# A written-out order of 1,052 steps changed in many small places, one unit's transposes moved to the DMA crossbar, and 18 idle memsets on GpSimd

## The chip, the cores and the metric

One Trainium2 chip, one core of it. The metric is the device time of the program in microseconds, as the median of several runs. One profiled execution of the kernel before is at hand, with a record of every instruction and DMA.

## The reference

Four sequences of 768 positions, 8 heads of 64. First attention in a window of 128 positions, with the first 4 positions ("sinks") always seen; then a channel mix (an FFN with a gate) on the heads laid side by side (512 wide).

```python
scores = scale * np.matmul(q, k.transpose(0, 1, 3, 2))
keep = is_sink | in_window          # rel in [0, 128), or position < 4
a = softmax(np.where(keep, scores, -1e9))
x = np.matmul(a, v)                 # then heads side by side: [4, 768, 512]

x_prev = x shifted by one position
xk = mu_k * x + (1.0 - mu_k) * x_prev
xr = mu_r * x + (1.0 - mu_r) * x_prev
k = np.maximum(xk @ w_k, 0.0)       # 512 -> 1024
v = k * k @ w_v                     # 1024 -> 512
r = 1.0 / (1.0 + np.exp(-(xr @ w_r)))
out = r * v
```

## The kernel before

**Units.** The work is cut into 12 units of 256 positions, three to a sequence (`u = 3 * b + T`). Each unit goes through the same steps. `load` brings k, q and v from HBM (two DMAs of 256 KB each) on the queue of SP. `prepare` casts k, q and v to bf16 and transposes k and q: with PE (`transpose`, then an `evacuate` copy out of PSUM by ACT or DVE) in the first units, with a DMA transpose on SP's queue (`turn`) where `KD` and `QD` say so, k from unit 4 and q from unit 8. `attend` makes the scores on PE in two pairs of head pairs, takes their exp on ACT (`expo`), multiplies by the window mask on DVE (`masked`; units 0 and 1 add a bias on PE instead), and multiplies by v on PE (`values`, 16 matmuls of 65 columns with two head pairs); DVE divides (`rec`, a reciprocal, and `x`). `sink_scores`, `es` and `sink_values` are the same for the four sink positions, whose keys GpSimd copies out of kt with `sink_keys` once a sequence. `mix` transposes x (`xtp` on PE and a copy, or two DMA transposes for the units in `XD`), forms the shifted difference `td` and from it `xk` and `xr` (four `stt` of 256 columns each). `ffn` of a unit makes `keys` (8 halves of 4 matmuls), `relu`, `square`, `gate` (2 of 4 matmuls, and a tanh), `product` (4 of 4 matmuls) and the output, which SP stores.

**What sets the order.** Nothing is scheduled at run time. Every step is put down with `P.op` under a running number. `ORDER` lists these numbers in the order in which the steps are issued; an engine runs its own steps in this order and waits for each. Numbers below zero are fillers: a matmul of 512 zero columns into a bank (`warm`, L1018), which nobody reads. `CHOICE` gives, by number, the engine for the steps that ACT, DVE or GpSimd can do. `SLOTS` gives, for each buffer taken, which of a pool's buffers it is. Weights are loaded whole (`load_weight`), and cast to bf16 by ACT or DVE (the `emit` steps for `wk`, `wr`, `wv`).

**Lines used below.** L337, L317, L307: loads of q and k (by 8 rows of descriptors or plain) and v; L354: weights; L536, L543: casts of k and q; L646: cast of v; L576: PE transposes of k and q; L589: their copies to kt and qt; L562: the DMA transposes `turn`; L670: `sink_keys`; L680: sink values; L703, L775: the two exps; L721, L728: scores and bias; L808: `values`; L849, L858, L869: x by PE, its copy, x by DMA; L877, L888: difference and mixes; L939, L979, L997, L909: `keys`, `gate`, `product`, the last product; L1006, L919: outputs; L1013: stores; L501: weight casts.

Of the kernel before, what the change touches and what calls it, by code (L numbers as in the profile page):

```python
# [8 lines left out]
FP32 = mybir.dt.float32  # L9
# [9 lines left out]
    92: "ACT", 93: "ACT", 94: "ACT", 95: "ACT", 97: "ACT", 100: "ACT", 102: "DVE", 105: "DVE",  # L19
    110: "DVE", 111: "DVE", 114: "ACT", 115: "DVE", 139: "POOL", 142: "POOL", 145: "POOL", 148:  # L20
    "DVE", 150: "DVE", 151: "ACT", 152: "ACT", 154: "DVE", 161: "DVE", 191: "DVE", 193: "DVE",
    194: "DVE", 197: "DVE", 199: "DVE", 200: "DVE", 203: "DVE", 204: "DVE", 213: "DVE", 230:
    "ACT", 234: "ACT", 273: "DVE", 276: "DVE", 279: "DVE", 282: "DVE", 285: "ACT", 286: "ACT",
    298: "DVE", 306: "DVE", 315: "ACT", 354: "DVE", 364: "ACT", 365: "DVE", 367: "DVE", 383:
    "ACT", 387: "ACT", 436: "DVE", 439: "DVE", 444: "DVE", 445: "DVE", 467: "ACT", 475: "ACT",
    514: "DVE", 516: "DVE", 521: "DVE", 524: "ACT", 525: "ACT", 546: "ACT", 550: "ACT", 554:
    "ACT", 558: "ACT", 595: "DVE", 598: "DVE", 603: "ACT", 604: "ACT", 606: "DVE", 634: "ACT",
    681: "DVE", 682: "DVE", 691: "DVE", 700: "ACT", 704: "ACT", 708: "ACT", 755: "DVE", 759:
    "DVE", 760: "ACT", 772: "DVE", 781: "ACT", 785: "ACT", 789: "ACT", 834: "DVE", 836: "DVE",
    837: "DVE", 853: "ACT", 856: "DVE", 857: "ACT", 860: "DVE", 861: "ACT", 904: "DVE", 906:  # L30
    "DVE", 910: "DVE", 912: "DVE", 913: "DVE", 929: "ACT", 933: "ACT", 940: "DVE", 941: "ACT",
    994: "DVE", 995: "ACT", 999: "ACT", 1003: "ACT", 1007: "ACT", 1022: "DVE", 1026: "DVE",
    1034: "DVE", 1035: "ACT",
# [5 lines left out]
XD = (9,10,11)  # L39
# [146 lines left out]
def kernel(  # L186
# [14 lines left out]
    nc = tc.nc  # L201
# [326 lines left out]
    def prepare(u, rank):  # L528
        b, T = divmod(u, NT)
# [545 lines left out]
```

## Time and profile before

| what | value |
|---|---|
| median of 3 runs | 166.04 us (165.84 to 166.12) |
| profiled execution, first to last instruction (span) | 164.3 us |
| own time of that execution, with what lies around the span | not given by itself; the median is 1.74 us above the span |
| PE busy (matmuls) | 158.4 us, 96% |
| DVE busy | 145.4 us, 89% |
| ACT busy | 131.2 us, 80% |
| GpSimd (POOL) busy | 13.5 us, 8% |
| mean granted TensorE clock | 0.999 |
| moved by DMA | 34.60 MB, mean 211 GB/s |

A busy share says how much of the span an engine worked, not whether anyone waited for it. A matmul's busy time holds the way through the array, so that matmuls close behind each other overlap and a busy PE can still have waits in it; the chain that ended last shows start to start instead. SPq stands for the queue of DMAs that SP issues, in order; such an instruction's length is the time of issue, and the landing comes later.

### The profile page before, as it was taken

To read this page: it belongs to the slowest core of one execution; us is meant where nothing else is said; L and a number is where in the kernel's file an instruction comes from. 1 tells how busy PE (TensorE), PEld (TensorE's weight loads), DVE (VectorE), ACT (ScalarE), POOL (GpSimd) and SP (SyncE) were. 2 spreads that over 40 slices of the span, in tenths; PEclk is the share of its full clock that TensorE was granted. 3 is DMA by queue.
4 is the path that set the end of the run, shared out by engine and by line. 5 is a ranking of instruction groups with operands and counts; after the bars stand their busy time and mean duration, and the time that the engine had idled before them with its cause. 6 is when DMAs were issued, how large, how long until landed. Compare 5 with 4: busy or idle time off the path is not lost.

```text
span 164.3 us, 4195 instructions
## 1 busy us (share of the span) xinstructions
PE 158.4 (96%) x1603; PEld 102.6 (62%) x1603; DVE 145.4 (89%) x381; ACT 131.2 (80%) x218; POOL 13.5 (8%) x38
## 2 busy tenths in 40 slices
PE   6999889999999999999999999999999999999992
PEld 2455568866467587577566775856575765664851
DVE  5259999999999999989999999999999999789752
ACT  3277999999999999999999999997668759163240
POOL 6409300010000000060000000000000000000000
PEclk9999999999999999999999999999999999999999
DMA  4999999999969896999999887986996955077743
GB/s 120 247 305 311 348 335 355 301 354 210 228 154 270 135 240 148 234 198 167 224 216 157 188 156 163 235 146 150 199 123 136 362 149 200 0 90 297 262 185 128
DMA packets 79042, 34.60 MB, mean 211 GB/s; under 512 B 67112, under 2 KB 73520, under 8 KB 79024
## 3 DMA queue, kind: packets, MB, share of 16 engines
q1 hardware_dynamic: 79008, 34.35, 86.3%
q8 instruction: 12, 0.20, 0.6%
q14 instruction: 6, 0.05, 0.1%
q10 hardware_dynamic: 16, 0.00, 0.0%
HBM read 24.12 MB, written 6.29 MB: 185 GB/s over the span
## 4 chain that ended last, share of the span: by engine, by line
PE 79%; ACT 8%; SPq 4%; DMA 3%; issue 2%; DVE 1%; POOL 1%; DVEq 0%; ACTq 0%; POOLq 0%
PE bank L997 23%; PE bank L939 23%; PE bank L979 12%; PE bank L808 6%; PE sc L721 6%; SPq L337 3%; DMA qs<-in_q_dram 3%; PE bank L576 2%; ACT e L775 2%; PE bank L849 2%; ACT rl L949 1%; PE bank L763 1%; ACT qt L589 1%; PE bank L909 1%; PE bank L1018 1%
## 5 line engine op out<-in xcount | busy, mean ns | idle before, releaser
L775 ACT ACTIVATE e<-sc 128x1024 bf16<-128x1024 f32 (+1 forms) x48 | 46.1, 994 | 1.8 <-PE sc L721 1.7
L939 PE MATMUL bank<-xk,wk_sb 128*128 128x256 bf16 x384 | 47.1, 273 | 0.0
L997 PE MATMUL bank<-wv_h,kk 128*128 128x512 bf16 x184 | 43.1, 379 | 0.1
L939 PEld LDWEIGHTS <-wk_sb 128*128 128x128 bf16 x384 | 36.4, 98 | 7.4 <-issue 0.4
L949 ACT ACTIVATE rl<-bank 128x512 bf16<-128x512 f32 x40 | 24.2, 625 | 8.6 <-PE bank L939 7.1
L997 PEld LDWEIGHTS <-kk 128*128 128x128 bf16 x184 | 17.1, 98 | 17.8 <-issue 0.4
L789 DVE TENSOR_TENSOR e<-e,mask 128x1024 bf16<-128x1024 bf16 (+1 forms) x40 | 25.4, 642 | 0.7 <-ACT e L775 0.5
L979 PE MATMUL bank<-wr_sb,xr 128*128 128x512 bf16 x96 | 23.7, 379 | 0.0
L888 DVE SCALAR_TENSOR_TENSOR xk<-td,mu_all,xt 128x256 bf16<-128x256 bf16 x48 | 22.4, 483 | 0.3
L888 DVE SCALAR_TENSOR_TENSOR xr<-td,mu_all,xt 128x256 bf16<-128x256 bf16 x48 | 22.1, 475 | 0.2
L967 ACT ACTIVATE kk<-rl 128x512 bf16<-128x512 bf16 x29 | 18.3, 664 | 4.2 <-DVE rl L953 4.0
L985 ACT ACTIVATE th<-bank 128x512 f32<-128x512 f32 x24 | 15.1, 646 | 5.7 <-PE bank L979 5.7
L825 DVE TENSOR_TENSOR x<-bank,rec 128x256 bf16<-128x256 f32 x48 | 19.2, 416 | 0.4
L808 PE MATMUL bank<-vb,e 128*128 128x65 bf16 x352 | 16.6, 194 | 0.0
L1006 DVE SCALAR_TENSOR_TENSOR w<-th,bank 128x512 f32<-128x512 f32 x19 | 13.0, 682 | 3.6 <-issue 1.8
L808 PEld LDWEIGHTS <-e 128*128 128x128 bf16 x352 | 13.6, 97 | 3.5
L979 PEld LDWEIGHTS <-xr 128*128 128x128 bf16 x96 | 8.8, 98 | 8.6 <-issue 0.2
L721 PE MATMUL sc<-qt,kt 64*128 64x128 bf16 (+1 forms) x256 | 13.9, 238 | 0.0
L721 PEld LDWEIGHTS <-kt 64*128 64x128 bf16 x256 | 8.9, 94 | 5.7 <-issue 3.1
L1018 PE MATMUL bank<-warm 128*128 128x512 bf16 x30 | 10.6, 484 | 1.1 <-DVE warm L1038 1.1
L877 DVE TENSOR_TENSOR td<-xt 128x512 bf16<-128x512 bf16 x24 | 10.3, 428 | 0.7 <-ACT xt L858 0.5
L589 ACT COPY qt<-bank 128x512 bf16<-128x512 bf16 x15 | 9.4, 643 | 1.0 <-PE bank L576 1.0
(74 smaller groups left out, 161.7 us busy)
## 6 DMA issues: line engine op xcount, KB each, us to landing
ks<-in_k_dram SPq DMA_DIRECT2D x24, 256.0 KB, 4.7
qs<-in_q_dram SPq DMA_DIRECT2D x24, 256.0 KB, 4.4
vs<-in_v_dram SPq DMA_DIRECT2D x24, 256.0 KB, 4.4
out_dram<-w SPq DMA_DIRECT2D x19, 256.0 KB, 2.7
w<-in_moe_w_k_dram SPq DMA_DIRECT2D x2, 1024.0 KB, 10.4
w<-in_moe_w_v_dram SPq DMA_DIRECT2D x2, 1024.0 KB, 9.3
w<-in_moe_w_r_dram SPq DMA_DIRECT2D x1, 1024.0 KB, 9.7
out_dram<-ob SPq DMA_DIRECT2D x4, 256.0 KB, 2.6
```

What stands on the lines that cost most here:

```text
L721: nc.tensor.matmul(out=sc[:, a, o0:o1], lhsT=lhs[rows], rhs=rhs[rows], start=u not in BIAS, stop=True, skip_group_check=u in BIAS)
L775: nc.scalar.activation(out=buf[ek][:, :, lo:], in_=buf[sck][:, :, lo:], func=AF.Exp, scale=scale)
L789: nc.vector.tensor_tensor(out=at, in0=at, in1=m, op=ALU.mult)
L808: nc.tensor.matmul(out=o[:, g, a, :], lhsT=e[:, a, e0:e0 + 128], rhs=rhs, start=(T == 0 and i == 0), stop=(i == len(blocks) - 1), skip_gro ...
L825: P.op("DVE", dve(256), lambda ok=ok, rk=rk, c=c: nc.vector.tensor_tensor(out=buf["x", u][:, :, 128 * c:128 * c + 128].rearrange("p g (a d ...
L888: nc.vector.scalar_tensor_tensor(out=buf[key][:, c, :], in0=buf[tk][:, i, :], scalar=mu[w][:, c:c + 1], in1=xt[:, c, t0 - 1:t0 + 255], op0 ...
L939: nc.tensor.matmul(out=ps[:, i, :], lhsT=wk_sb[:, c, 128 * f:128 * f + 128], rhs=xk[:, c, :], start=(c == 0), stop=(c == NC - 1), skip_gro ...
L949: nc.scalar.activation(out=buf[rk], in_=buf[psk].rearrange("p (i t) -> p i t", i=2), func=AF.Relu)
L967: nc.scalar.activation(out=buf["kk", u][:, 2 * f2:2 * f2 + 2, :], in_=buf[rk], func=AF.Square)
L979: nc.tensor.matmul(out=buf[psk], lhsT=buf["xr", u][:, c, 128 * g:128 * g + 128], rhs=wr_sb[:, c, :], start=(c == 0), stop=(c == NC - 1))
L985: P.op("ACT", act(512), lambda psk=psk, tk=tk: nc.scalar.activation(out=buf[tk], in_=buf[psk], func=AF.Tanh, scale=0.5), rank + 4 + g, tak ...
L997: nc.tensor.matmul(out=buf[psk], rhs=wv_h[:, f, :], lhsT=buf["kk", u][:, f, 128 * g:128 * g + 128], start=(f == 0), stop=(f == NF - 1))
```

## The change

Three things are changed.

1. `XD` goes from units 9, 10, 11 to units 8 to 11: x of unit 8 is transposed by two DMA transposes in place of two packs of four PE transposes with a copy each. That makes 1,050 steps of 1,052.
2. `ORDER`, `CHOICE` and `SLOTS` are replaced. Decoded to step names: 19 fillers in place of 30. In units 0 and 1, q is loaded ahead of k, and the steps of q stand ahead of those of k. Before unit 0's first `keys`, the new order has the first score pair of unit 2, the second half of unit 1's x transposes and the second half of unit 2's k transposes, which came after it; unit 2's sink scores came before and come after. Engines change for 60 steps: v of units 0 and 1 and a part of q of unit 1 go to GpSimd (5 casts); counted over all, ACT has 225 steps in place of 219, DVE 356 in place of 369. Loads move by a few places on SP's queue; v of unit 11's first half is loaded much earlier. Near the end, the last `values` (unit 11) stand ahead of both gates and all products of unit 9; both gates of unit 11 stand ahead of its keys, and the four products of unit 10 behind them.
3. `sink_keys` of the second sequence (unit 3) is followed by 18 memsets of one column each into a tile that nothing reads.

```diff
 CHOICE = {
-    92: "ACT", 93: "ACT", 94: "ACT", 95: "ACT", 97: "ACT", 100: "ACT", 102: "DVE", 105: "DVE",
...
+    92: "DVE", 93: "ACT", 94: "ACT", 95: "ACT", 96: "DVE", 97: "ACT", 98: "DVE", 99: "DVE", 100:
+    "ACT", 101: "DVE", 102: "DVE", 104: "ACT", 105: "DVE", 107: "ACT", 108: "ACT", 110: "DVE",
+    111: "ACT", 113: "ACT", 114: "POOL", 115: "POOL", 139: "POOL", 141: "ACT", 142: "POOL", 144:
+    "ACT", 145: "POOL", 147: "ACT", 148: "POOL", 150: "ACT", 151: "POOL", 152: "POOL", 154: "DVE",
...
-XD = (9,10,11)
+XD = (8, 9, 10, 11)
...
 ORDER = (
-    80, 81, 78, 82, 87, 83, 84, 77, -1, -2, -3, -4, -1, -2, 90, 0, 1, 79, 102, 108, -2, -3, -4,
-    -2, -3, -4, -2, 103, 104, 2, 3, 119, 105, -3, -4, 106, 107, 109, 110, 4, 5, 114, -2, -2, -2,
-    120, 121, 115, -2, -3, -4, -2, -3, 122, 111, 112, 123, 124, 125, 126, 127, 129, 113, 130,
...
+    80, 82, 83, 87, 86, 77, 2, 85, 3, 0, 1, 4, 5, 81, 88, 114, 78, -1, -2, -3, -4, -1, 119, 8, 79,
+    105, -2, -3, -4, 106, 102, 107, 111, 89, 115, -4, -2, -3, -4, -1, 112, 108, -3, -4, 103, 104,
+    -4, -1, 120, 109, 121, -3, 90, 91, 117, 118, 125, 113, 122, 123, 110, 9, 129, 84, 126, 130,
...
+    spare = tile1([128, 18], FP32, "spare")
...
             for a in range(2):
                 rows = slice(64 * a, 64 * a + 64)
                 nc.gpsimd.tensor_copy(out=kz[rows, :, 4 * a:4 * a + NS],
                                       in_=first(rows))
+            if b == 1:
+                for i in range(18):
+                    nc.gpsimd.memset(spare[:, i:i + 1], 0.0)
```

More of the change, by code (lines that the diff above doesn't have):

```diff
@@ L18 @@
 CHOICE = {
-    92: "ACT", 93: "ACT", 94: "ACT", 95: "ACT", 97: "ACT", 100: "ACT", 102: "DVE", 105: "DVE",
[L20 to L30, printed above, removed]
@@ L31 @@
-    "DVE", 910: "DVE", 912: "DVE", 913: "DVE", 929: "ACT", 933: "ACT", 940: "DVE", 941: "ACT",
-    994: "DVE", 995: "ACT", 999: "ACT", 1003: "ACT", 1007: "ACT", 1022: "DVE", 1026: "DVE",
-    1034: "DVE", 1035: "ACT",
+    92: "DVE", 93: "ACT", 94: "ACT", 95: "ACT", 96: "DVE", 97: "ACT", 98: "DVE", 99: "DVE", 100:
+    "ACT", 101: "DVE", 102: "DVE", 104: "ACT", 105: "DVE", 107: "ACT", 108: "ACT", 110: "DVE",
+    111: "ACT", 113: "ACT", 114: "POOL", 115: "POOL", 139: "POOL", 141: "ACT", 142: "POOL", 144:
@@ new lines @@
+    "ACT", 145: "POOL", 147: "ACT", 148: "POOL", 150: "ACT", 151: "POOL", 152: "POOL", 154: "DVE",
+    161: "DVE", 191: "DVE", 193: "ACT", 194: "DVE", 196: "ACT", 197: "DVE", 199: "ACT", 200:
+    "ACT", 202: "ACT", 203: "DVE", 204: "DVE", 206: "DVE", 213: "DVE", 221: "ACT", 222: "ACT",
+    225: "DVE", 226: "DVE", 229: "ACT", 230: "ACT", 233: "DVE", 234: "DVE", 273: "DVE", 275:
+    "ACT", 276: "DVE", 278: "ACT", 279: "DVE", 281: "ACT", 282: "DVE", 284: "ACT", 285: "ACT",
+    286: "ACT", 291: "ACT", 298: "ACT", 306: "ACT", 307: "DVE", 310: "ACT", 311: "DVE", 314:
@@ new lines @@
+    "ACT", 315: "ACT", 318: "ACT", 319: "DVE", 354: "DVE", 356: "ACT", 358: "ACT", 359: "ACT",
+    361: "ACT", 363: "ACT", 364: "ACT", 365: "ACT", 367: "DVE", 374: "ACT", 382: "ACT", 383:
+    "ACT", 386: "ACT", 387: "DVE", 390: "ACT", 391: "DVE", 394: "ACT", 395: "DVE", 434: "ACT",
+    436: "DVE", 438: "ACT", 439: "DVE", 441: "ACT", 443: "ACT", 444: "DVE", 445: "DVE", 447:
+    "ACT", 454: "DVE", 462: "ACT", 463: "ACT", 466: "ACT", 467: "ACT", 470: "ACT", 471: "DVE",
+    474: "ACT", 475: "ACT", 514: "DVE", 516: "DVE", 518: "ACT", 519: "ACT", 521: "ACT", 523:
@@ new lines @@
+    "ACT", 524: "DVE", 525: "DVE", 530: "DVE", 537: "ACT", 545: "ACT", 546: "ACT", 549: "ACT",
+    550: "ACT", 553: "ACT", 554: "ACT", 557: "ACT", 558: "ACT", 593: "DVE", 595: "DVE", 597:
+    "ACT", 598: "DVE", 600: "ACT", 602: "ACT", 603: "ACT", 604: "ACT", 606: "ACT", 613: "ACT",
+    621: "ACT", 622: "ACT", 625: "ACT", 626: "DVE", 629: "ACT", 630: "DVE", 633: "ACT", 634:
+    "DVE", 673: "ACT", 675: "ACT", 677: "DVE", 679: "ACT", 681: "DVE", 682: "ACT", 684: "ACT",
+    691: "DVE", 699: "ACT", 700: "DVE", 703: "ACT", 704: "ACT", 707: "DVE", 708: "DVE", 711:
@@ new lines @@
+    "ACT", 712: "DVE", 751: "ACT", 753: "ACT", 755: "ACT", 757: "ACT", 759: "ACT", 760: "ACT",
+    778: "ACT", 779: "DVE", 782: "ACT", 783: "ACT", 786: "ACT", 787: "ACT", 790: "ACT", 791:
+    "ACT", 826: "DVE", 828: "ACT", 830: "DVE", 832: "ACT", 834: "ACT", 835: "ACT", 850: "ACT",
+    851: "ACT", 854: "ACT", 855: "DVE", 858: "ACT", 859: "ACT", 862: "ACT", 863: "ACT", 902:
+    "ACT", 904: "ACT", 906: "ACT", 908: "DVE", 910: "DVE", 911: "ACT", 926: "ACT", 927: "ACT",
+    930: "ACT", 931: "ACT", 934: "ACT", 935: "ACT", 938: "ACT", 939: "ACT", 992: "ACT", 993:
@@ L34 @@
+    "ACT", 996: "ACT", 997: "ACT", 1000: "DVE", 1001: "DVE", 1004: "ACT", 1005: "ACT", 1020:
+    "ACT", 1021: "ACT", 1024: "DVE", 1025: "DVE", 1028: "ACT", 1029: "ACT", 1032: "ACT", 1033:
+    "DVE",
 }
```

151 rows, old and new, of tables (ORDER, SLOTS) are left out of this document.

## The prediction

> **What bounds the kernel now.** I read the page's busy shares first, then busy time by stretch, then the chain that ended last, then instructions in order of time at both ends.
>
> ```profile
> span 164.3 us, 4195 instructions
> PE 158.4 (96%) x1603; PEld 102.6 (62%) x1603; DVE 145.4 (89%) x381; ACT 131.2 (80%) x218; POOL 13.5 (8%) x38
> ```
>
> ```profile
> 8.00:16.00 8.00, 7.70 (x84) 4.36 (x82) 5.65 (x17) 5.98 (x11) 3.36 (x6) 1.00 1.06 305
> 16.00:24.00 8.00, 7.04 (x113) 4.67 (x113) 7.93 (x24) 7.69 (x13) 1.87 (x8) 1.00 1.10 343
> 24.00:32.00 8.00, 8.00 (x88) 6.92 (x88) 7.79 (x21) 8.00 (x13) 0.00 (x0) 1.00 1.07 319
> 60.00:73.00 13.00, 12.94 (x153) 9.48 (x150) 12.25 (x31) 12.94 (x24) 2.50 (x2) 1.00 0.89 192
> 120.00:130.00 10.00, 10.00 (x96) 6.50 (x95) 9.76 (x23) 6.78 (x12) 0.00 (x0) 1.00 0.76 195
> 150.00:161.00 11.00, 11.00 (x76) 7.14 (x73) 7.38 (x15) 2.91 (x5) 0.00 (x0) 1.00 0.54 202
> ```
>
> The stretch table's columns are the stretch, its length, busy time of PE, PEld, DVE, ACT and POOL, the granted clock, the DMA share, GB/s. From 24 us to the end PE is busy 8.00 of 8.00, 10.00 of 10.00, 11.00 of 11.00; the weakest stretch, 60 to 73, still has 12.94 of 13.00. There is nothing to win there except less PE work. ACT is just as full up to 73 and then empties (6.78 of 10, 2.91 of 11). Only the first 24 us have room on PE.
>
> ```profile
> 7.97 4.54 DMA qs<-in_q_dram
> 12.64 0.88 POOL qb L543
> ...
> 18.51 0.59 ACT kt L589
> 19.10 0.29 ACT es L703
> 19.39 0.48 ACT qt L589
> ...
> 20.33 0.88 issue
> ...
> 24.13 0.90 PE bank L939 x8
> 25.03 0.22 PE bank L849 x4
> 25.25 0.22 PE bank L576 x4
> ...
> 26.47 0.55 PE sc L721 x12
> ...
> 157.63 1.73 PE bank L997 x8
> 159.36 1.76 PE bank L909 x16
> 161.15 0.42 DVE w L919
> ```
>
> This is the chain that ended last (start, length, what). Up to 24.13 it walks through the DMA of unit 1's q, a GpSimd cast and ACT copies, so the opening is bound by arrivals and by the in-order queues of ACT, DVE and GpSimd. From 24.13 (first FFN product, `keys`) PE carries nearly all of it, to 161.15. The rest, 3.1 us, is the last DVE operation and the store. The span is 164.3 and the median of the runs 166.04; I take the 1.74 between them as fixed. So the time moves with two things: when PE starts its FFN work, and how much PE work and PE waiting lie behind that.
>
> **The change part by part.**
>
> *Fillers.* The new order has 19 filler matmuls instead of 30.
>
> ```profile
> 1.13 2.74 PE L1018 MATMUL bank<-warm 128*128 128x512 bf16 x6 [1.13 <-DVE warm L1038]
> 4.17 3.03 PE L1018 MATMUL bank<-warm 128*128 128x512 bf16 x7
> 9.97 1.25 PE L1018 MATMUL bank<-warm 128*128 128x512 bf16 x5
> 16.68 1.94 ACT L775 ACTIVATE e<-sc 128x1024 bf16<-128x1024 f32 x2 [0.31 <-PE sc L721]
> 21.84 0.29 PE L696 MATMUL bank<-qt,ksink 128*32 128x256 bf16 x4 [0.50 <-ACT qt L589]
> 22.85 1.08 ACT L501 ACTIVATE wk_sb<-w 128x1024 bf16<-128x1024 f32 x1
> ```
>
> One filler takes 0.22 us late (5 in 1.25, with the pipeline's tail) and 0.43 early (7 in 3.03): the array starts at half rate and is at full rate by about 7 us, though the granted-clock column says 1.00 throughout. The new order keeps 18 ahead of unit 0's `values`, so the warm-up stays; those left out stood after it, in time when PE waits anyway: 0 us for the work itself. The cover that is lost is activity: gaps like the 0.50 in the row above will be longer, up to about 1 us, the length of one exp (1.94 for two). The upper end is a slow-clock rival below; I take 0. [...]
>
> *Work moved ahead of the first FFN product.* Before, the transposes of x of unit 1's second half (0.22, at 25.03), of k of unit 2's second half (0.22) and the first score pair of unit 2 (0.55) come behind the first `keys`. In the new order all three come ahead, and unit 2's sink scores (four matmuls; its packs of four cost PE the 0.22 of the other packs of four) go behind. PE work behind the first FFN product: -0.22 - 0.22 - 0.55 + 0.22 = **-0.77 us**.
>
> *x of unit 8 by the crossbar.* Two packs of four PE transposes go: **-0.44 us** of PE, and two ACT copies with them. SP gets two DMA transposes. Their price on SP and their delay are those of units 9 to 11:
>
> ```profile
> L869 SPq DMA_TRANSPOSE xt<-x x6: 1189/1230/2405, 117.3 to 144.0; - x6
> DMA to landing us min/median/max: 2.5/3.5/4.2
> ```
>
> 1.23 us of issue each. Between unit 8's last `values` and its first `keys` the new order lays 13 us of PE work (11.2 before); the way now needed is about 2.5 (reciprocals and x) + 5.1 (both transposes, from the tail below) + 2.3 for the first operations on DVE: it fits. Queued behind these transposes on SP are the loads of q and k of unit 11 and of v of unit 10; unit 11's k transposes follow behind unit 9's x transposes as well, and by the median landing they are down about 1.3 us before unit 11's scores are due (2.7 before). I take 0, with a rival.
>
> *The first units, q ahead of k.* The whole opening is changed: q0, k0, v0, q1, k1 are loaded in this order (before k0, q0, v0, half of k1, q1, rest of k1), v0 and v1 and all four casts of unit 1 go to GpSimd, and DVE and ACT get other pieces. Unit 1's q has one 256 KB load less ahead of it: at the 305 GB/s of the stretch 8 to 16 that is 0.9 us on its landing at 12.5 (an estimate). Its transposes feed the first exp of unit 1, at 16.68; I take 0.5 us earlier. From that exp on ACT is the chain, in its own order: two exps 1.94, k copy 0.59, k copy 0.48, sink exp 0.29, k copy 0.48, two exps 1.94, q cast 0.48, q copy 0.48, sum 6.7; then scores 0.55, a transpose 0.22, a filler 0.22, hand-over 0.1: 7.8 us, against 24.13 - 16.68 = 7.45 before. First FFN product: -0.5 + 0.35 = **-0.15 us**. Below, it is bound by w_k, whose first cast starts at 22.85 without waiting: at most 1 us earlier. Above, by GpSimd (first rival): +2.75.
>
> *Unit 1's keys earlier.* A mix is one of these:
>
> ```profile
> L888 DVE SCALAR_TENSOR_TENSOR xk<-td,mu_all,xt 128x256 bf16<-128x256 bf16 x48 | 22.4, 483 | 0.3
> ```
>
> In the new order the keys of unit 1 start 2.0 us of PE work behind the first product, not 3.7. Their inputs come from DVE: x of unit 1 at about 22.9 (first exp at 16.2 and the 6.7 of ACT's order), a w_k cast now on DVE, some 0.7, then copy, difference and four mixes, by 22.4 us for 48 mixes 0.47 each and rather less for the other two, 2.6: 26.2. The slot is 24.0 + 2.0 = 26.0. Bounds 0 to 0.9 (if x comes as late as PE's own work lets it); taken **+0.3 us**.
>
> *Choices by engine.* ACT gets 6 instructions more, DVE 13 fewer, GpSimd 5 casts more.
>
> ```profile
> L646 ACT CAST vb<-vs 128x512 bf16<-128x512 f32 x11 | 7.6, 692 | 0.0
> L646 DVE CAST vb<-vs 128x512 bf16<-128x512 f32 x13 | 5.4, 420 | 0.1
> L543 POOL CAST kb<-ks 128x512 bf16<-128x512 f32 x2 | 1.4, 702 | 0.0
> L670 POOL COPY ksink<-kt 64x16 bf16<-64x16 bf16 x8 | 4.0, 501 | 75.2 <-DMA kt<-kb 60.4 <-ACT kt L589 14.6
> L1056 POOL MEMSET const-float32-1.0<- 128x1 f32 x1 | 0.1, 109 | 0.0
> ```
>
> By these rows ACT gains about 6 x 0.65 = 4 us, but units 5 to 8 lose a net eight ACT operations and the additions lie in units 8 to 11, where ACT is at 6.78 of 10. PE being full in both, I take 0, and a cover lost only if DVE (9.76 of 10 there) falls behind; in the order, it has no more work ahead of any unit's last x than before.
>
> *18 memsets.* 0.109 us each, at most 2.0 us of GpSimd, after unit 3's sink keys. Nothing waits behind them on GpSimd until unit 6's sink keys (the 2.50 of POOL in the stretch 60 to 73). If every one held up DVE it would cost 2.0 us of DVE; if none, 0. Taken 0.
>
> *The tail.* Gates of unit 11 now stand ahead of its keys and before the products of unit 10.
>
> ```profile
> 139.88 0.40 PE L808 MATMUL bank<-vb,e 128*128 128x65 bf16 x8
> 142.79 3.65 SPq L869 DMA_TRANSPOSE xt<-x  x2
> 147.27 0.69 DVE L1006 SCALAR_TENSOR_TENSOR w<-th,bank 128x512 f32<-128x512 f32 x1 [0.60 <-PE bank L997]
> 147.88 0.42 DVE L877 TENSOR_TENSOR td<-xt 128x512 bf16<-128x512 bf16 x1
> 152.25 3.66 PE L939 MATMUL bank<-xk,wk_sb 128*128 128x256 bf16 x32
> ```
>
> From the end of the last `values` (140.28) to the first difference of unit 11 it takes 7.6 us. DVE then needs two differences (0.42), an output (0.69) and six mixes (0.47), 4.3, less some overlap, about 4, until the gate's last input: 11.6. The new order gives PE six products and gates (0.86 each), eight key halves (0.44) and two gates between: 10.4 us (12.0 before, to 152.25, unit 11's keys first). Between 0, if the transposes land after 2.5, and 1.3; the last input is needed by the third of four matmuls, so **+0.5 us**.
>
> Sum: -0.77 - 0.44 - 0.15 + 0.3 + 0.5 = **-0.56 us**: span 163.7, time 166.04 - 0.56, about **165.5 us**.
>
> **The rivals.** (1) *GpSimd is late: slower.* Unit 0's second k copy now stands on DVE behind a reciprocal, which needs `values`, which need both v casts, now on GpSimd behind two masks. Then unit 1's four casts follow there. A cast takes 0.70 by the row, but the pair of tiny sink-key copies in the stretch 60 to 73, where DVE was busy 12.25 of 13, took 2.50. If the five added casts take 1.25 each, as one of that pair on average, the opening is 5 x 0.55 = 2.75 us late: -0.56 + 2.75 gives 168.2; at half, 166.9. It decides for slower from 0.56 + 0.33 = 0.9 us of lateness. For it: DVE is 7.93 of 8 busy at 16 to 24. Against: DVE gives up work there. [...]
> (2) *Nothing gained.* The work taken ahead only fills PE time which the fillers filled, and the first product comes as much later as there is less behind it: 166.0. For it: the ACT sum of 7.8 against 7.45.
> (3) *More gained.* The product starts with w_k, 1 us earlier, and neither tail nor unit 1 waits: -0.77 - 0.44 - 1.0: 163.8.
> (4) *A transfer or the clock.* Unit 11's k lands late behind two sets of transposes, or the opening drops to half rate for 3 us: +1 to +3, about 167.5. Little speaks for it.
>
> **How the numbers follow.** About 0.2% (0.33 us) is what a measurement of this kernel can tell from no change. My forecast (164.4 to 165.7) 0.41, more gained 0.14, nothing gained 0.18, GpSimd late 0.2, transfer or clock 0.07. Faster 0.55, same 0.18, slower 0.27. The forecast's own range is 164.4 to 165.7; with (2), (3) and the nearer half of (1) and (4) the range is 163.8 to 167.3.
>
> **What would show it.** The first L939 matmul at 23.5 to 24.3; PE full from there; eight L849 matmuls fewer; L1018 19 times; a PE wait of 0.3 to 1.3 before the last L979 pair; xt transposes 8 times on SP. Wrong would be: POOL's casts over 1 us and the first L939 after 25; a PE gap over 1 us between 30 and 140; L997 or L939 spacing doubled near 15 to 24.

## The result and the profile after

The changed kernel takes 164.63 us (median of 20 runs, 163.65 to 166.04), the kernel before 166.04 in the runs beside it: ratio 0.9919, 95% interval 0.9898 to 0.9940. Repeated later as e5, beside fresh runs of the kernel before, it took 165.17: ratio 0.9959, interval 0.9936 to 0.9982. So the gain is 0.7 to 1.3 us by these two ratios (0.3 to 1.7 with their intervals), and a single run of it strays more than one of the kernel before. Two profiles below are of executions slower than the rest, that of e3 (TensorE at half pace throughout) and that of e8; the ratios leave such runs out.

Line numbers have moved: `keys` is L956 (before L939), `gate` L996, `product` L1014, the last product L926, scores L738, `values` L825, x by PE L866, x by DMA L886, PE transposes L590 and their copies L603, casts of q and k L557, of v L660, w_k's casts L515 (ACT) and L521 (DVE), exps L792, fillers L1035. In the runs below the same lines stand a few lines further up or down.

The page of the changed kernel, its head:

```profile
span 163.3 us, 4148 instructions
...
PE 155.3 (95%) x1565; PEld 101.0 (62%) x1584; DVE 139.5 (85%) x368; ACT 133.6 (82%) x224; POOL 16.6 (10%) x61
```

Busy time by stretch, columns as in the prediction:

```profile
8.00:16.00 8.00, 7.18 (x87) 4.22 (x86) 4.83 (x14) 5.55 (x9) 5.33 (x12) 1.00 1.07 281
16.00:24.00 8.00, 6.57 (x107) 4.54 (x108) 7.74 (x24) 7.35 (x12) 1.25 (x2) 1.00 0.95 329
24.00:32.00 8.00, 8.00 (x77) 6.30 (x78) 7.93 (x19) 8.00 (x13) 0.00 (x0) 1.00 1.14 325
60.00:73.00 13.00, 12.89 (x148) 9.28 (x147) 12.57 (x34) 12.87 (x23) 2.68 (x2) 1.00 0.99 221
110.00:120.00 10.00, 9.43 (x78) 4.92 (x78) 8.98 (x25) 8.78 (x15) 0.00 (x0) 1.00 0.95 161
```

Between 8 and 24 us PE is busy 13.75 us instead of 14.74; the fillers left out were idle time before. From 24 us on it is nearly full again, with one hole that stands out, 0.57 us between 110 and 120. The chain that ended last, at both ends:

```profile
22.15 0.62 ACT qb L557
22.77 0.50 ACT qt L603
23.31 0.62 PE sc L738 x12
23.95 0.40 PE bank L866 x4
24.34 0.21 PE bank L1035
24.56 0.60 PE bank L956 x4
25.16 0.22 PE bank L713 x4
25.38 5.01 PE bank L956 x44
...
147.29 2.59 PE bank L996 x12
...
160.33 0.42 DVE w L936
```

The first key product starts at 24.56 (before: 24.13). From it to the last DVE operation it takes 160.33 - 24.56 = 135.77 us (before: 161.15 - 24.13 = 137.02). So 0.43 us is lost ahead and 1.25 won behind. The key products run on from 25.38 without a wait for unit 1, and unit 11's gates at 147.29 do not wait either.

### The profile page after: what moved, and what is told of

It is laid out like the page before. It is cut to its first block, busy times and chain, and to the rows that moved or that the text cites. A ratio compares the mean times of both kernels' runs of the same rounds, so it can differ in the third digit from the quotient of the medians.

```text
span 163.3 us, 4148 instructions
## 1 busy us (share of the span) xinstructions
PE 155.3 (95%) x1565; PEld 101.0 (62%) x1584; DVE 139.5 (85%) x368; ACT 133.6 (82%) x224; POOL 16.6 (10%) x61
## 4 chain that ended last, share of the span: by engine, by line
PE 84%; DVE 4%; DMA 3%; issue 3%; ACT 2%; SPq 1%; ACTq 0%; DVEq 0%
PE bank L956 24%; PE bank L1014 22%; PE bank L996 13%; PE sc L738 7%; PE bank L825 6%; DMA vs<-in_v_dram 3%; PE bank L590 3%; PE bank L1035 3%; PE bank L866 2%; PE sc L745 1%; PE bank L780 1%; PE bank L926 1%; DVE x L842 1%; PE bank L713 1%; SPq L576 1%
## 5 line engine op out<-in xcount | busy, mean ns | idle before, releaser
L956 PE MATMUL bank<-xk,wk_sb 128*128 128x256 bf16 x384 | 47.7, 273 | 0.1
L792 ACT ACTIVATE e<-sc 128x1024 bf16<-128x1024 f32 (+1 forms) x48 | 45.2, 968 | 2.9 <-PE sc L738 2.8
L1014 PE MATMUL bank<-wv_h,kk 128*128 128x512 bf16 x169 | 42.4, 379 | 0.7
L956 PEld LDWEIGHTS <-wk_sb 128*128 128x128 bf16 x384 | 36.1, 98 | 7.9 <-DVE wk_sb L521 0.3
L966 ACT ACTIVATE rl<-bank 128x512 bf16<-128x512 f32 x43 | 25.4, 613 | 4.4 <-PE bank L956 4.0
L1014 PEld LDWEIGHTS <-kk 128*128 128x128 bf16 x184 | 16.9, 98 | 17.1 <-issue 0.2
L996 PE MATMUL bank<-wr_sb,xr 128*128 128x512 bf16 x92 | 23.5, 379 | 0.7 <-ACT rl L966 0.5
L905 DVE SCALAR_TENSOR_TENSOR xk<-td,mu_all,xt 128x256 bf16<-128x256 bf16 x48 | 21.9, 477 | 0.1
L1002 ACT ACTIVATE th<-bank 128x512 f32<-128x512 f32 x24 | 14.4, 625 | 5.3 <-PE bank L996 5.2
L984 ACT ACTIVATE kk<-rl 128x512 bf16<-128x512 bf16 x28 | 17.3, 639 | 0.1
L825 PE MATMUL bank<-vb,e 128*128 128x65 bf16 x352 | 16.2, 194 | 0.5 <-ACT e L792 0.5
L825 PEld LDWEIGHTS <-e 128*128 128x128 bf16 x352 | 13.8, 97 | 4.2 <-ACT e L792 0.8
L738 PE MATMUL sc<-qt,kt 64*128 64x128 bf16 (+1 forms) x256 | 14.0, 238 | 0.7 <-DVE kt L603 0.3
L996 PEld LDWEIGHTS <-xr 128*128 128x128 bf16 x96 | 8.8, 98 | 9.2 <-issue 0.8
L1023 DVE SCALAR_TENSOR_TENSOR w<-th,bank 128x512 f32<-128x512 f32 x17 | 11.6, 681 | 2.4 <-PE bank L1014 1.9
L738 PEld LDWEIGHTS <-kt 64*128 64x128 bf16 x256 | 9.1, 94 | 6.4 <-issue 2.7
L603 ACT COPY qt<-bank 128x512 bf16<-128x512 bf16 x16 | 9.7, 605 | 3.4 <-PE bank L590 3.2
L684 POOL COPY ksink<-kt 64x16 bf16<-64x16 bf16 x8 | 4.8, 604 | 73.5 <-DMA kt<-kb 34.0
```

What stands on the lines that cost most here:

```text
L738: nc.tensor.matmul(out=sc[:, a, o0:o1], lhsT=lhs[rows], rhs=rhs[rows], start=u not in BIAS, stop=True, skip_group_check=u in BIAS)
L792: nc.scalar.activation(out=buf[ek][:, :, lo:], in_=buf[sck][:, :, lo:], func=AF.Exp, scale=scale)
L825: nc.tensor.matmul(out=o[:, g, a, :], lhsT=e[:, a, e0:e0 + 128], rhs=rhs, start=(T == 0 and i == 0), stop=(i == len(blocks) - 1), skip_gro ...
L905: nc.vector.scalar_tensor_tensor(out=buf[key][:, c, :], in0=buf[tk][:, i, :], scalar=mu[w][:, c:c + 1], in1=xt[:, c, t0 - 1:t0 + 255], op0 ...
L956: nc.tensor.matmul(out=ps[:, i, :], lhsT=wk_sb[:, c, 128 * f:128 * f + 128], rhs=xk[:, c, :], start=(c == 0), stop=(c == NC - 1), skip_gro ...
L966: nc.scalar.activation(out=buf[rk], in_=buf[psk].rearrange("p (i t) -> p i t", i=2), func=AF.Relu)
```

## The experiments

All ratios are to the kernel before, run beside each. "Behind the product" is the time from the first key product to the last DVE operation in the profile; 135.77 in the changed kernel, 137.02 before.

**e1, the moved work moved back.**

```diff
 ORDER
-    ... 185, 207, 249, 186, 92, 212, 93, 213, 208, 214, -2, 219, 215, 247, 220, 223, 209 ...
+    ... 185, 207, 186, 92, 93, 208, 219, 247, 220, 249, 212, 213, 214, 215, 223, 209 ...
```

Here 249 is the score pair of unit 2, 212 the x transpose of unit 1, 219 and 220 the first two key halves.

> The changed kernel with the moved work moved back: the scores of unit 2 (0.62 us of TensorE) and the second x transpose of unit 1 (0.22) stand behind the first two key halves of unit 0 again, and the filler ahead of them (0.21) goes. Moved-work theory: the first key product cannot start before w_k is there (its transfer landed at 23.7, the VectorE cast of 0.68 ends at 24.5), so TensorE idles where the moved work stood and everything ends 0.62 + 0.22 = 0.84 us later than in the changed kernel: 164.63 + 0.84 = 165.5, and a TensorE gap of about 1 us ends at the first key product at 24.5. Rival (the order of these two steps is worth nothing, the first key product starts earlier by as much): the first key product at 23.5 to 23.7, 164.6. Rival (unit 1 is then late): more than 0.84, 166 or above, with a wait ahead of unit 1's keys.

166.88 us, ratio 1.0039 [1.0006, 1.0072]; e4, run beside it and equal to the changed kernel in time, has 0.9957. So 0.0082 x 166 = 1.4 us slower by the ratios, whose intervals leave room for about 0.7 us either way. PE in order of time:

```profile
24.38 0.61 PE L958 MATMUL bank<-xk,wk_sb 128*128 128x256 bf16 x4 [1.47 <-DVE wk_sb L523]
...
28.13 4.12 PE L958 MATMUL bank<-xk,wk_sb 128*128 128x256 bf16 x31 [0.52 <-DVE xk L907]
```

PE idles 1.47 us for w_k's cast where the moved work had stood, and 0.52 us for unit 1's mixes, which are now late: both the theory and the third reading are at work. How the time divides between them is not shown. This execution took 165.98 us and ends its last DVE operation 0.93 us behind that of the first profile of the changed kernel and 1.15 behind that of e4. Three of the executions in the ratio had a lower mean granted clock (0.98 to 0.99) and took 168.0 to 168.4, which no execution of e4 did (0.998 or more); without these three the difference of the medians is near the 0.84 of the theory. In this order the moved work fills a wait for w_k's cast.

**e2, x of unit 8 by PE again.**

```diff
-XD = (8, 9, 10, 11)
+XD = (9, 10, 11)
```

The two packs of PE transposes and their copies stand about 2 us of PE work behind unit 8's last x.

> The changed kernel with x of unit 8 transposed by TensorE again (8 more transposes, two more evacuations on ScalarE, two transposing transfers fewer), all else in the same order. Theory (TensorE sets the end here): 8 x 0.055 = 0.44 us more, 165.07. Rival (the transposes stand beside a wait, as at 111 us, and cost nothing): 164.6. Rival (the gain is in what the DMA queue gives up or takes on: two transposing transfers fewer on the queue let the loads behind them start about 2.4 us earlier and the wait at 111 us goes): 164.5 or less.

166.64 us, ratio 1.0033 [1.0009, 1.0057]: 0.0076 x 166 = 1.3 us slower than e4, more than any theory gave. PE in order of time:

```profile
111.32 0.38 PE L869 MATMUL bank<-ident,x 128*128 128x128 bf16 x4 [0.51 <-ACT rl L969]
112.38 0.38 PE L869 MATMUL bank<-ident,x 128*128 128x128 bf16 x4 [0.67 <-ACT xt L878]
```

Beside the 0.44 us of work stand 1.18 us of waits: the first pack waits for a relu on ACT, the second for ACT's copy of the first. With the DMA transposes of the changed kernel PE waits 0.52 us there in the first profile (for a relu on ACT, before 111.99), and not at all near 111 us in e4 and e5. Where this order puts them, PE transposes cost three times their own length (1.3 us against 0.44); at another place they might cost less.

**e3, the second half of v of unit 9 earlier.**

```diff
 ORDER
-    ... 63, ... 71, ... 829, ... 75, 827, 64 ...
+    ... 63, 64, ... 71, ... 829, ... 75, 827 ...
```

This answers a wait that I had not foreseen, in the changed kernel's chain and in its ACT and PE in order of time:

```profile
105.42 5.38 DMA vs<-in_v_dram
```

```profile
110.82 0.62 ACT L660 CAST vb<-vs 128x512 bf16<-128x512 f32 x1 [2.56 <-DMA vs<-in_v_dram]
```

```profile
111.99 1.02 PE L996 MATMUL bank<-wr_sb,xr 128*128 128x512 bf16 x4 [0.52 <-ACT rl L966]
```

> The changed kernel with one load moved in the queue's order: the second half of v of unit 9 right behind its first half, ahead of a half of k and of v of unit 11 and two transposing transfers (from 105.4 us to about 101.5 us). Theory: ScalarE's wait of 2.56 us for it (until 110.8) goes, and with it the TensorE gap of 0.52 us before 112.0: 164.63 - 0.5 = 164.1, and a smaller spread from run to run if that landing is what varies. Rival (the gap is taken back by slack behind it): 164.6.

Ratio 0.9938 [0.9911, 0.9966], against 0.9957 of e4: 0.3 us, within both intervals, so not shown. In the profiles of e4 and e5 ACT waits for the same load, 1.30 and 0.77 us, but PE has no hole near 111 us. The hole comes and goes, and may be one part of the spread.

**e4, no memsets.**

```diff
-            if b == 1:
-                for i in range(18):
-                    nc.gpsimd.memset(spare[:, i:i + 1], 0.0)
```

> The changed kernel without the 18 memsets. Theory: they lie on an idle GpSimd (0.11 us each, 2 us in all near 36 us) and delay nobody: 164.6 (within 0.2%). Rival (they hold up VectorE or shift the sink keys behind them usefully): a difference of up to 2.0 us of VectorE work near 36 us, time moved by 0.5 us or more either way.

165.32 us, 0.9957 [0.9932, 0.9982], the same as e5 with them (0.9959). As far as these intervals can tell, the 18 are free.

**e5, the changed kernel again** (no edit).

> The changed kernel itself once more, as the measure for the kernels run beside it and for its own spread. Theory (the spread comes from when the loads of the first 15 us land and from the load of v of unit 9 that ScalarE waits for at 108 to 111 us): median 164.6 to 165.3, single runs 163.6 to 166.1; in its profile the first key product lies between 24.4 and 25.2, and what follows it takes 135.0 us without the wait near 111 us and 135.8 with it. Rival (spread on the chip as a whole): the kernel before spreads as widely.

165.17 us (164.89 to 167.13), the kernel before 165.97 (165.50 to 166.51). Its chain:

```profile
25.16 0.60 PE bank L956 x4
...
160.48 0.42 DVE w L936
```

Behind the product 135.32 us, without the hole near 111 but with one of 0.31 near 57 us for another cast of v. The first key product is 0.6 us later than in the first profile: 24.56, 24.90 (e2), 25.16 (e4) and 25.16, with the same steps ahead of it; what this goes with stands further down. The kernel before spreads by 1.0 us, this one by 2.2; the rival of a spread of the whole chip falls.

**e6, ten times the memsets.**

```diff
-                for i in range(18):
-                    nc.gpsimd.memset(spare[:, i:i + 1], 0.0)
+                for i in range(180):
+                    nc.gpsimd.memset(spare[:, i % 18:i % 18 + 1], 0.0)
```

> The changed kernel with 180 memsets in place of 18. Theory (they run on an idle engine and hold nobody up): GpSimd has 162 x 0.11 = 17.8 us more work from 36 to about 54 us, done before unit 6's sink keys (60 us and later): the time of the changed kernel within 0.2%, DVE's operations beside them no longer. [...]

171.65 us, ratio 1.0341 [1.0312, 1.0370]: 6.5 us slower than e5. GpSimd and DVE in order of time, then two stretches:

```profile
35.35 6.22 POOL L688 MEMSET spare<- 128x1 f32 x180
```

```profile
35.86 6.00 DVE L557 CAST qb<-qs 128x512 bf16<-128x512 f32 x1
```

```profile
38.00:40.00 2.00, 0.00 (x0) 0.00 (x0) 2.00 (x1) 0.00 (x0) 2.00 (x65) 1.00 1.18 311
42.00:44.00 2.00, 2.00 (x8) 0.92 (x9) 2.00 (x6) 0.59 (x1) 0.00 (x0) 0.50 0.93 223
```

One cast on DVE, 0.42 us elsewhere, takes 6.00 us and ends at 41.86, when the train of memsets (35.35 + 6.22 = 41.57) is through. PE stands still with it for 5.3 us and comes back at half the clock (0.50). The theory is refuted as a general one: a memset costs 6.22 / 180 = 0.035 us, but here the train of them held a DVE operation until it was over. In the changed kernel the train is 0.69 us long, and the cast beside it took 0.47.

**e7, the opening alone.** Order and engines of the changed kernel up to the first key product, then those of the kernel before. Unit 2's sink scores stay ahead of the first product, as in the kernel before.

```diff
-ORDER = before
+ORDER = after's steps up to 219 (first keys), then before's for the steps not yet issued
```

> The kernel before with the changed kernel's order and engines up to unit 0's first key product (and its 19 fillers), and its own order and engines for all that is left; x of unit 8 by TensorE, no memsets. Work of TensorE behind the first key product by the groups' durations: 136.65 in the kernel before, 135.66 here. Moved-work theory: 0.99 us less behind it, and the first key product 0.3 to 1.0 us later than the 24.1 of the kernel before: 166.1 - 0.99 + 0.3 to 1.0 = 165.5 to 166.1. Rival (the opening gains nothing, the gain is in the choices and order of the middle): 166.1 or more. Rival (the opening is the whole gain): 164.6 to 164.9.

167.95 us, ratio 1.0118 [1.0105, 1.0132]: slower than either kernel. The first key product starts at 25.91, and there is a wait behind it:

```profile
28.53 2.79 PE L940 MATMUL bank<-xk,wk_sb 128*128 128x256 bf16 x24 [0.76 <-ACT wk_sb L502]
```

ACT has the cast of the next part of w_k behind a relu that waits for these very keys. Behind the product it takes 162.66 - 25.91 = 136.75, only 0.27 less than before where 0.99 less work stands. So the new opening in front of the old middle gained nothing here: its product comes 0.75 to 1.35 us later than in the changed kernel, and ACT's next cast waits in the wrong place behind it.

**e8, w_k first**, meant to be better than both.

```diff
 ORDER
-    ... 12, ... 13, 19, 20, ... 10 ...          (q of unit 2, then w_k)
+    ... 12, ... 13, 10, 19, 20 ...              (w_k, then q of unit 2)
-    ... 185, 207, 249, 186, 92, 212, 93, ... -2, 219, 215, 247, 220 ...
+    ... 92, 219, 220, 185, 207, 249, 186, 212, 93, ... 215, 247 ...
```

with e3's edit.

> A version meant to be better: the changed kernel with the first half of w_k issued ahead of q of unit 2, its cast on VectorE ahead of the last reciprocal of unit 1, the first two key halves of unit 0 ahead of the scores of unit 2, the last filler out, and the second half of v of unit 9 loaded right behind its first. Theory (the first key product is set by w_k's landing at 23.7 us, and TensorE idles 0.9 to 1.4 us between 16 and 24): the key product starts near 22.9, 0.5 us of idle time is filled, and the wait near 111 us is gone: 0.5 to 1.0 us less than the changed kernel. Rival (the loads of the opening share one bandwidth, so q of unit 2 comes 3 us later and its scores wait): equal or slower than the changed kernel, with a TensorE wait of about 1 us for the q copies of unit 2.

166.48 us, ratio 1.0011 [0.9993, 1.0030]. The rival was right in its time and in its wait for q of unit 2, 1.04 us; a DMA share of 1.05 at 376 GB/s around it is as far as the run shows a shared bandwidth. Chain, PE, and two stretches of an execution that took 167.91 us:

```profile
15.81 6.78 DMA qs<-in_q_dram
```

```profile
23.16 0.40 PE L592 MATMUL bank<-ident,qb 128*128 128x128 bf16 x4 [1.04 <-DVE qb L559]
```

```profile
22.00:24.00 2.00, 0.96 (x20) 0.79 (x17) 1.29 (x5) 1.58 (x3) 0.00 (x0) 1.00 1.05 376
25.00:26.00 1.00, 1.00 (x5) 0.73 (x6) 0.68 (x3) 1.00 (x2) 0.00 (x0) 0.50 1.07 251
```

Behind 1 MB of w_k, q of unit 2 needs 6.78 us to land. PE, idle half the time from 22 to 24, drops to clock 0.50, and the first keys, at 24.99, run at half rate (8 matmuls in 1.89 us, 0.90 in the kernel before). The half rate of this execution explains none of the ratio; the load of q that comes late is the order's own.

**e9, GpSimd's casts given back.**

```diff
-    114: "POOL", 115: "POOL", 148: "POOL", 151: "POOL", 152: "POOL"
+    114: "ACT", 115: "DVE", 148: "DVE", 151: "ACT", 152: "ACT"
```

> The changed kernel with the five casts of units 0 and 1 that the change gave to GpSimd back on the engines of the kernel before (three to ScalarE, two to VectorE), at the same places in the order. Theory (on GpSimd they take 0.61 to 0.69 us each and nobody waits for them, and ScalarE and VectorE are the chain to the first key product): 3 x 0.5 = 1.5 us more on ScalarE and 2 x 0.33 = 0.7 us on VectorE, partly in their idle time before 16 us: the first key product 0.3 to 1.0 us later than the changed kernel's, 165.2 + 0.3 to 1.0 = 165.5 to 166.2. Rival (GpSimd was the late one, as my prediction's first rival had it): faster than the changed kernel, 164.6 or less. Rival (their idle time takes all of it): 165.2.

168.48 us, ratio 1.0107 [1.0068, 1.0146]: some 2.5 us slower than the changed kernel at 0.9957 to 0.9959. ACT, PE, and a stretch:

```profile
8.68 0.62 ACT L663 CAST vb<-vs 128x512 bf16<-128x512 f32 x1 [6.02 <-DMA vs<-in_v_dram]
```

```profile
9.93 0.38 PE L1038 MATMUL bank<-warm 128*128 128x512 bf16 x1 [2.37 <-ACT qt L606]
```

```profile
10.00:12.00 2.00, 1.85 (x10) 1.01 (x10) 0.00 (x0) 0.91 (x2) 0.61 (x1) 0.56 1.00 311
```

It is not mainly the 2.2 us of cast work. The cast of v stands at the head of ACT's queue until v lands at 8.68; the copy of q and the casts of q and k behind it wait, PE idles 2.37 us, and the clock falls to 0.56. The first key product starts at 29.12. Of the six executions, the four with a mean granted clock of 0.99 took 168.4 to 168.8 us and the two at 0.999 took 166.9 and 167.1: so some 1.6 us goes with the clock, and some 1.4 with the waits alone. In the changed kernel GpSimd waits for the same load, and no other engine stands still for it (the longest wait of PE from 7 to 12 us is 0.25, for a copy on ACT):

```profile
8.51 0.61 POOL L660 CAST vb<-vs 128x512 bf16<-128x512 f32 x1 [1.77 <-DMA vs<-in_v_dram]
```

**e10, 11 more fillers.** Three each behind the first transposes of q and the first scores, two behind the first x transposes, one ahead of unit 1's second sink values, two ahead of the first keys.

```diff
-    ... 120, 109, ... 249, ... -2, 219 ...
+    ... 120, f, f, f, 109, ... 249, ... -2, f, f, 219 ...      (f: a filler; 30 in all)
```

> The changed kernel with 11 more filler matmuls ahead of the first key product (30 as in the kernel before), put where TensorE mostly waits. Theory (TensorE waits in the opening for loads and casts, so fillers there cost little): 0 to 0.4 us for the two just ahead of the first key product, 165.2 to 165.6. Rival (the gain of the change is the 11 fillers left out): 11 x 0.22 = 2.4 us more at the most, 166 or above. Rival (more fillers bring the clock up sooner): 164.8 or less, with the spacing of the fillers at 0.22 before 6.2 us.

165.55 us, ratio 0.9955 [0.9936, 0.9975]: the changed kernel's. Put into an opening that waits for loads, these fillers cost nothing that can be measured, and leaving them out brings nothing.

**e11, only unit 8's x by the crossbar, on the kernel before.**

```diff
-XD = (9,10,11)
+XD = (8,9,10,11)
 ORDER: the two DMA transposes right behind unit 8's last x, its differences and mixes
        4 us of PE work later, its second gate behind its keys
```

> The kernel before with x of unit 8 transposed by the DMA crossbar and nothing else but what it needs: the differences and mixes of unit 8 some 4 us later, the second gate of unit 8 behind its keys. Theory (TensorE sets the end): 8 x 0.055 = 0.44 us less, 165.6. Rival (the two transposing transfers push the loads and turns behind them, as at 111 us in the changed kernel, and TensorE waits): 166.0 or more, with a TensorE wait of 0.4 us or more between 100 and 125 us. Rival (ScalarE and VectorE, relieved of two evacuations, were the limit there): more than 0.6 us, below 165.4.

175.77 us, ratio 1.0571 [1.0545, 1.0598]. SP's queue, then PE, then a stretch:

```profile
103.81 1.69 SPq L562 DMA_TRANSPOSE kt<-kb  x1
110.80 2.50 SPq L869 DMA_TRANSPOSE xt<-x  x2
```

```profile
117.93 0.40 PE L696 MATMUL bank<-qt,ksink 128*32 128x256 bf16 x4 [2.79 <-DMA qt<-qb]
...
121.24 0.82 PE L721 MATMUL sc<-qt,kt 64*128 64x128 bf16 x10 [2.59 <-DMA kt<-kb]
```

```profile
118.00:120.00 2.00, 0.66 (x6) 0.14 (x5) 0.49 (x3) 0.38 (x1) 0.00 (x0) 0.50 0.92 203
```

SP issues in order, and put right behind x these transposes hold its queue from 105.5 to 110.8 us. The load of k and the turns behind are issued at 113.34 and 114.02 instead of 105.44 and 107.10 in the kernel before; PE waits 2.79 and 2.59 us, and the granted clock is 0.50 between the two. My placing did this, so the run prices a bad place in the queue, not the crossbar. In the changed kernel the two transposes stand 4 us of PE work behind x, and the queue is rearranged around them.

**e12, the engines of the kernel before** behind the first key product.

```diff
-CHOICE: after's, for the steps behind 219
+CHOICE: before's, for the steps behind 219 (28 from ACT to DVE, 21 from DVE to ACT)
```

> The changed kernel with the engines of the kernel before for everything behind the first key product (49 operations of ScalarE and VectorE change places, 28 one way, 21 the other), order and opening as changed. Theory (in the kernel before the chain of waits runs over ScalarE from 59.7 to 73.1 us, and the TensorE work in these 13.18 us adds up to 12.73: 0.45 us of small waits that the changed choices took away, which my prediction put at 0): 0.4 to 0.8 us more than the changed kernel, 165.6 to 166.0, with ScalarE in the chain of waits between 60 and 73 us. Rival (engine choices are worth nothing, TensorE being full): 165.2.

173.30 us, ratio 1.0431 [1.0395, 1.0467], far past my 0.4 to 0.8 us. A stretch of it:

```profile
140.00:160.00 20.00, 17.77 (x119) 10.28 (x119) 13.96 (x35) 7.64 (x14) 0.00 (x0) 0.91 0.53 185
```

PE waits many times between 60 and 152 us, and DVE and ACT make up 36% of the chain that ended last, against 9% in the kernel before. Order and engines are fitted to each other: the choices of one order in another cost ten times what I had put them at, or more. The run shows that they matter; it does not price the 0.45 us.

## Why the prediction was right in sign and short in size

I gave 165.5 us, a gain of 0.56. That is less than the first measurement (1.41; interval 1.0 to 1.7) and inside the interval of the second (0.3 to 1.1). By steps:

- **First key product, -0.15: the step that failed.** It came 0.43 us later in the first profile and 0.77 to 1.03 in e2, e4 and e5. Unit 1's first exps did come earlier, as I had it (16.04, before 16.68). But my sum of 7.8 us from there let ACT run without a wait. ACT's own work was right to 0.1 us; what I left out is a wait of 0.62 for unit 1's second pair of scores, which are late because PE, in its order, waits ahead of them for DVE's x and for DVE's copy of its transposes. PE and ACT of the changed kernel:

```profile
17.52 0.40 PE L866 MATMUL bank<-ident,x 128*128 128x128 bf16 x4 [0.46 <-DVE x L842]
18.43 0.38 PE L590 MATMUL bank<-ident,kb 128*128 128x128 bf16 x4 [0.52 <-DVE xt L875]
```

```profile
20.33 1.94 ACT L792 ACTIVATE e<-sc 128x1024 bf16<-128x1024 f32 x2 [0.62 <-PE sc L738]
```

  The chain that ended last goes this way, over DVE, PE and ACT to the scores at 23.31. w_k is a second bound close behind. It had been moved behind q of unit 2 on SP's queue (issued at 15.22 instead of 13.56), and its cast stands late in DVE's order:

```profile
23.81 0.68 DVE L521 CAST wk_sb<-w 128x1024 bf16<-128x1024 f32 x1
```

  It ends at 24.49, and holds up PE for the last 0.15 us, behind the filler at 24.18. DVE shows no wait ahead of this cast; only in e1, where PE is there early, does the chain go through the transfer of w_k, which lands at 23.60.

  The same path goes with the spread of the opening. In e5 DVE waits for a load of unit 1's k:

```profile
15.85 0.43 DVE L557 CAST kb<-ks 128x512 bf16<-128x512 f32 x1 [0.39 <-DMA ks<-in_k_dram]
```

  This cast starts at 15.03 in the first profile, at 15.59 in e2, 15.84 in e4 and 15.85 in e5, and the first product at 24.56, 24.90, 25.16 and 25.16.
- **Moved work, -0.77: right.** Counted in the two traces, 12 score matmuls, 4 transposes of k and 12 of x (8 of them unit 8's) fewer stand behind the first product, and 4 sink scores more: that is the work of this term and the next, 1.21 us. Moving back the scores and the x transposes alone cost about 0.8 to 1.4 us (e1).
- **x of unit 8, -0.44: right in sign, worth more here,** 1.3 us against PE transposes at e2's place.
- **Unit 1's keys, +0.3: not there.** A wait for these mixes shows only in e1 (0.52). My term assumed x as late as the slot; it came in time because the product came later.
- **The tail, +0.5: not there.** In the changed kernel's DVE the difference starts at 143.62 and the last input of the gates ends at 147.49:

```profile
143.62 0.43 DVE L894 TENSOR_TENSOR td<-xt 128x512 bf16<-128x512 bf16 x1 [0.49 <-DMA xt<-x]
...
147.01 0.48 DVE L905 SCALAR_TENSOR_TENSOR xr<-td,mu_all,xt 128x256 bf16<-128x256 bf16 x1
```

  From the last `values` (137.75) this is 9.7 us, not my 11.6: x and its transposes took 5.9 to the difference instead of 7.6, and the chain shows the twelve gate matmuls at 147.29 without a wait.
- **Fillers, 0: right** (e10). That the longer gaps leave the clock up was an estimate, and no run shows how long a gap may be; in the profile of the changed kernel the longest wait of PE between its first matmul and the first key product is 0.52 us, not the 1 us I allowed, and the granted clock is given as 1.00 there. **Memsets, 0: right** for 18 (e4), at 0.035 to 0.038 us each, not 0.109. That memsets can cost DVE time, as my bound of 2.0 us allowed, e6 shows: one cast of 6.00 us beside 180 of them.
- **GpSimd's casts, 0 with a rival on the slow side: not late.** They took 0.62 us, not 1.25, and in the new order taking them away costs 2.5 us (e9). I weighed only how long a cast takes, not who waits behind one that waits for its load. What they bring against the kernel before, where ACT and DVE made these casts in another order, e9 does not show.
- **Engines and order behind the product, 0: too little in two of three profiles.** A full busy column hid waits of PE: the record of a key matmul is 273 ns long on average, where 28 of them take 3.07 us in the chain, 110 ns each. Counted from each matmul's start to the next one's, beyond what the same pair usually takes, PE of the kernel before waits 1.0 us in all behind its first key product. The changed kernel waits 1.1 us in the first profile (0.68 of it in the hole near 111), 0.35 in e4 and 0.7 in e5. From 59.7 to 73.1 us the chain of the kernel before runs over ACT, and in e4 it stays on PE; but by this count PE waits only 0.3 us there, not the 0.45 that e12 was to test. No run says how much of it is order and how much engines.

For e5 the sum is: 1.03 lost ahead; behind, 1.21 of work (my 0.77 and 0.44) and 0.3 to 0.4 of waits gained. That gives about -0.55, and the profile shows 160.48 - 161.15 = -0.67, the medians -0.80. The first profile and e4 come out the same way, with some 0.15 us left open in each.

That the time lies within my range is in part luck. I had put in 0.8 us for unit 1's keys and the tail that was not there, and had left out 0.6 to 1.2 us ahead of the first product that was.

Of the rivals, "GpSimd late" and "a transfer or the clock" did not happen, though e9, e11 and e6 show waits and clock losses of these kinds in neighbours of this kernel. "Nothing gained" had half of it: 0.4 to 1.0 us of what was won behind the product was lost ahead of it. "More gained" (163.8) is about as far from the first measurement (164.63) as my 165.5 is; neither the unit nor the tail waited, as it had it, but the product did not come earlier.

## What to carry to other kernels

When an opening waits for loads, follow every input of the first dear step back, weights included, and ask of each engine on the way what it waits for in its own order; a sum of one engine's work leaves the waits out. A cast that waits for a transfer belongs on an engine with nothing behind it; in e9 its duration of 0.62 us said little, beside its wait of 6.02 us at the head of ACT's queue and the 2.37 us that PE idled. Order, engine choice and queue order are one design: three edits that took one part out of the changed kernel or into the old one (e7, e11, e12) ended up to 9.5 us slower than the kernel they were meant to explain.

## What was not expected of the hardware

- **A train of tiny GpSimd memsets held up a DVE cast.** 6.00 us instead of 0.42 (e6); it ends at 41.86, the train at 41.57. A product on DVE beside the first memsets, at 35.55, still took 0.39. The cast came through only behind the last of 180 instructions, not between two of them. In which way the train held it is not shown; the trace shows the cast's length and its end.
- **The clock fell after less idleness than I allowed for.** My sum let the gaps of the opening grow to 1 us at no cost, as an estimate, and I gave a fall of the clock little weight. After waits of 2.37 us (e9) and 2.79 us (e11) the granted clock is 0.56 and 0.50. In the profiled execution of e8 it is 0.86 from 24 to 25 us and 0.50 from 25 to 28, with PE busy 1.39 us of the three from 22 to 25 and no single wait over 1.04.
- **An execution can stay at half pace from start to end.** In e3's profile the span is 312.8 us and a key matmul takes 445 ns on average instead of 273 (records that overlap; the 384 of them keep PE busy 96.4 us, where they take 47.7 in the changed kernel), PE being busy 97%, while the granted clock is given as 1.00:

```profile
L959 PE MATMUL bank<-xk,wk_sb 128*128 128x256 bf16 x384 | 96.4, 445 | 0.4 <-issue 0.4
```

  Its steps are the changed kernel's but for one load. One run of e1 took 315 us as well, none of the kernel before did; whether the new opening makes it likelier is not settled by so few.
